# A gated mix of sliding attention and a squared-ReLU MLP on one core: start addresses of split operands moved to 64 modulo 256

## The chip, the cores and the metric

The kernel runs on one core of one Trainium2 chip. A core has TensorE (PE in the profile, its weight loads as PEld), VectorE (DVE), ScalarE (ACT), GpSimd (POOL) and SyncE (SP, which issues the transfers). They share an on-chip memory of 128 partitions; a tile occupies the same byte range in each partition, and "start address" below is that byte offset. The metric is the device time of one execution in microseconds (us); for the kernel before it is the median of three runs.

## The reference

For a sequence of 2,048 tokens of width 448, with one head block A and one MLP block B on the same x, the reference computes

```
g = sigmoid(sum(x * gate_w))                       # one number per token
q, k, v = x @ wqkv                                 # 16 heads of 28
logits  = q . k over the 8 positions s, s-2, ..., s-14, scaled by 28**-0.5
a = softmax(logits) . v  @ wo
b = relu(x @ w1 + b1)**2 @ w2 + b2                 # 448 -> 1792 -> 448
out = g * a + (1 - g) * b
```

All of it is in 32-bit floating point.

## The kernel before, in words

**Split operands.** Each matmul operand is split into a high part, which the matmul format holds exactly, and a low part, the rest. Each product is then three matmuls: high by high, high by low and low by high. ACT writes the high parts (a copy into the format), DVE subtracts to get the low ones. The tiles with h and l in their names are these parts: w1h and w1l, w2ah and w2al, and so on; for x, one tile holds both, the low part 2,048 bytes behind the high one.

**Side by side.** The width 448 is three blocks of 128 rows and one of 64. `side_by_side` (line 308) takes two lists of products and issues them alternately, one on partitions 0 to 63 and one on partitions 64 to 127, so that two half-height matmuls are in work at a time. Nearly all matmuls are issued at its line 315. In `nc.tensor.matmul(out, a, w)` the second argument is the stationary operand (it is loaded into the array, 128 columns) and the third is the moving one (it streams through, 448, 450 or 512 columns).

**Stages.** Tokens are in four chunks of 512.

- QKV (`qkv_first` and `qkv_two`, from line 393): for chunks 0, 1, 2, 3 in turn, x is stationary and wqkv moves, 448 columns for k and v and 450 for q (two more for the gate). Chunk 0 has a start of its own (line 402, matmuls over all 128 partitions). Results go to DRAM. Two pieces of the MLP are woven into the end of chunk 3.
- MLP: for chunks 3, 0, 1, 2 in turn (`ORDER`) and for 14 blocks of 128 hidden units taken two at a time, the h products (w1 stationary, x moving, 512 columns; `h_first`, `h_second`) and the b products (h stationary, w2 moving, 448 columns; `o_part`). For each later chunk, x is brought back from DRAM into tiles of `xpool` and one more slot in the pool `bw` (`x_reload`).
- Attention: POOL multiplies q by k and the weights by v, DVE reduces the products (the "pp" tiles of `prodp`), beside the MLP on PE.
- Output projection: the o tiles stationary, wo moving (`wo_split`, `wo_first`, `wo_second`, `wo_end`), woven into the MLP and at its end.

**Order of the work.** Instructions are put in order by a planner in Python (`Plan`) from fixed costs and due times; it knows nothing of addresses. SP issues nearly all transfers, in the planner's order.

**Where tiles lie.** Pools are laid out one behind the other in the order in which they are opened, and tiles within a pool likewise. The first tile of the pool `const` starts at byte 1,152, which is 128 modulo 256. Most tiles have a size that is a multiple of 256 bytes, so the remainder is handed on from tile to tile until a small tile of 64 or 192 bytes changes it. In the kernel before there are four such places: the gates' tile zg (192 bytes, between the pools `prodp` and `rawp`), b1z (64 bytes), and the tiles pad_a and pad_b (192 bytes each, never used). The slice `[:, 48:48 + n * P]` in `wo_split` skips 192 bytes as well. Remainders of the operands of PE, modulo 256:

| operand | role | before | after |
|---|---|---|---|
| wqkv parts | moving in QKV | 128 | 128 |
| x of chunks 0 and 2 | stationary in QKV | 64 | 64 |
| x of chunks 1 and 3 (pool xpool) | stationary in QKV | 128 | 64 |
| x of all chunks in the MLP (xpool, slot in bw) | moving in h | 128 | 64 |
| w1 and w17 parts | stationary in h | 128 | 64 |
| h parts | stationary in b | 64 | 64 |
| w2a and w2b parts | moving in b | 128 | 128 |
| o parts | stationary in the output projection | 64 | 64 |
| wo parts | moving in the output projection | 128 | 128 |

Every slice that a matmul takes begins a multiple of 256 bytes into its tile, so the remainder of the tile is that of the operand.

Of the kernel before, what the change touches and what calls it, by code (L numbers as in the profile page):

```python
# [7 lines left out]
F32 = mybir.dt.float32  # L8
F32R = mybir.dt.float32r
# [4 lines left out]
S, D, H, DH, W, F = 2048, 448, 16, 28, 8, 1792  # L14
P = 128
NS = 8
# [4 lines left out]
C = HG * DH  # L21
NF = F // P
# [15 lines left out]
PP_BUFS = 4  # L38
# [15 lines left out]
class Plan:  # L54
# [29 lines left out]
    def add(self, eng, cost, fn, *deps, prio=MID, at=0.0, port=False, move=None):  # L84
        j = Job()
        j.eng, j.cost, j.fn, j.deps, j.prio, j.port, j.move = eng, cost, fn, [d for d in deps if d], prio, port, move
        j.at, j.done, self.count = max(at, self.now), None, self.count + 1
        j.n = self.count
        self.jobs[eng].append(j)
        return j  # L90
# [88 lines left out]
def gated_mix_kernel(ctx: ExitStack, tc: tile.TileContext, xT, wqkv, w1, w2, wo, b1, b2, out):  # L179
    nc = tc.nc  # L180

    def f32(ap):
        return ap.bitcast(F32)
# [12 lines left out]
    const = ctx.enter_context(tc.tile_pool(name="const", bufs=1))  # L196
    psum = ctx.enter_context(tc.tile_pool(name="psum", bufs=1, space=bass.MemoryType.PSUM))

    w1h = const.tile([P, 3, F], F32R, name="w1h")
    w1l = const.tile([P, 3, F], F32R, name="w1l")  # L200
    w17h = const.tile([P, F // 2], F32R, name="w17h")
    w17l = const.tile([P, F // 2], F32R, name="w17l")
    NFA = NF // 2
    w2ah = const.tile([P, NFA, D], F32R, name="w2ah")
    w2al = const.tile([P, NFA, D], F32R, name="w2al")
    b2t = const.tile([P, D], F32, name="b2t")
    mask = const.tile([P, NS, W], F32, name="mask")

# [1 line left out]
    attp = ctx.enter_context(tc.tile_pool(name="attp", bufs=1))  # L210
    smp = ctx.enter_context(tc.tile_pool(name="smp", bufs=2))
    prodp = ctx.enter_context(tc.tile_pool(name="prodp", bufs=1))
    smallp = ctx.enter_context(tc.tile_pool(name="smallp", bufs=1))
    zg = smallp.tile([P, 6, NS], F32, name="zg")
    zt, gt, g1t = zg[:, 0:2], zg[:, 2:4], zg[:, 4:6]
    rawp = ctx.enter_context(tc.tile_pool(name="rawp", bufs=2, reuse_waits="tile"))
    biasp = ctx.enter_context(tc.tile_pool(name="biasp", bufs=1))
# [26 lines left out]
    def dma(fn, packets, size, *deps, prio=MID, at=0.0):  # L244
        return add(SYNC, 430.0, fn, *deps, prio=prio, at=at, move=(packets, size))
# [639 lines left out]
    def w2hl(f):  # L885
        if f < NFA:
            return w2ah[:, f], w2al[:, f]
        return w2bh[:, f - NFA], w2bl[:, f - NFA]

# [44 lines left out]
    bw = ctx.enter_context(tc.tile_pool(name="weights_b", bufs=1, reuse_waits="tile"))  # L934
    bp = ctx.enter_context(tc.tile_pool(name="phase_b", bufs=1, reuse_waits="tile"))
    w2bh = bw.tile([P, NFA, D], F32R, name="w2bh")
    w2bl = bw.tile([P, NFA, D], F32R, name="w2bl")
    woh = bw.tile([P, 3, D], F32R, name="woh")
# [6 lines left out]
    def x_reload(i, j, slot):  # L945
        c = ORDER[i]
        xt = (xpool if slot < 4 else bw).tile([P, 2, CH], F32R, tag=f"x{slot}", name=f"x{c}b_{j}")
        job = dma(lambda: nc.sync.dma_start(f32(xt), x_d[c, j]), 128, 4096, plan.after_pe(), x_stored[c][j], prio=NEXT)
        nxt[j] = (xt, slot, job)

    x_reload(1, 3, 4)
    bw.tile([P, 48], F32, name="pad_b")

# [23 lines left out]
    def fin_fetch(par, t):  # L979
        if (par, t) in half:  # L980
            fin_begin(par, t)
# [51 lines left out]
    def wo_split(par, t, hold, loads):  # L1033
        st = Wo()
        st.par, st.t = par, t
        place = "pp" if par and t % 4 else "oh"
        st.place = place
        free = part_last["oh"] if place == "oh" else reduced_all[-PP_BUFS:] + part_last["pp"]
        st.accs = accs = [Acc("m", f"a{par}_{t + r}", D, now=False) for r in range(2)]

        def parts():
            if place == "pp":
                oh, ol, o78 = (prodp.tile([P, C * W], F32R, tag="pp", name=f"o{n}{par}_{t}", bufs=PP_BUFS)[:, 48:48 + n * P]
                               for n in (6, 6, 2))
            else:
                oh, ol, o78 = (bp.tile([P, n * P], F32R, tag=tag, name=f"{tag}{par}_{t}")
                               for tag, n in (("oh", 6), ("ol", 6), ("o7", 2)))
            st.oh, st.ol = (o.rearrange("p (k t n) -> p k t n", k=3, t=2) for o in (oh, ol))
            st.o7, st.o8 = o78[:, :P], o78[:, P:]
            raw = hold[0]  # L1050
            st.full, st.last = raw[:, :6 * P].rearrange("p (k t n) -> p k t n", k=3, t=2), raw[:, 6 * P:]
            nc.scalar.activation(st.oh, st.full, AF.Copy)

        def copied(r):
            accs[r].open()
            st.pv = getattr(st, "pv", []) + [accs[r].pt.rearrange("p (k n) -> p k n", k=4)]
            nc.scalar.activation(st.pv[r][:, 0:3], st.full[:, :, r], AF.Copy)

        a = add(ACT, 847.0, parts, *loads, *free, prio=SOON)
        b = [add(ACT, 486.0, lambda r=r: copied(r), a, *accs[r].after, prio=SOON) for r in range(2)]  # L1060
        b[1].deps.append(b[0])
        c7 = add(ACT, 293.0, lambda: nc.scalar.activation(st.o7, st.last, AF.Copy), b[1], prio=SOON)
        d7 = add(ACT, 262.0, lambda: nc.scalar.activation(st.pv[0][:, 3], st.last, AF.Copy), c7, prio=SOON)
        lows = [add(DVE, 550.0, lambda r=r: nc.vector.tensor_sub(st.ol[:, :, r], st.pv[r][:, 0:3], f32(st.oh[:, :, r])),
                    b[r], prio=SOON) for r in range(2)]
        lows.append(add(DVE, 280.0, lambda: nc.vector.tensor_sub(st.o8, st.pv[0][:, 3], f32(st.o7)), d7, prio=SOON))
        if not par or t == 0:
            raw_last["ot"] = [d7]
        for r in range(2):
            fin_fetch(par, t + r)  # L1070
        st.jobs = [d7, *lows]
        accs[0].after, accs[1].after = (*st.jobs,), (*st.jobs,)
        return st
# [119 lines left out]
    for g in range(2, 2 * NF):  # L1193
        i, f = g // (NF // 2), g % (NF // 2) * 2
# [111 lines left out]
```

## Time and profile before

| | |
|---|---|
| median of the runs | 415.89 us (415.61 to 416.22, 3 runs) |
| the profiled execution | 415.95 us, its span 414.1 us |
| mean granted TensorE clock | 0.999 |
| PE busy | 408.6 us |
| POOL, DVE, ACT busy | 265.8, 258.6, 206.0 us |

The span runs from the first to the last instruction of the one profiled execution; its time holds a little more, what lies around the span. All times within the profile count from the span's start. An engine's busy time is the sum of the stretches in which it had an instruction in work; matmuls overlap, so the pace of PE is read from how many start in a stretch of time, and not from the duration of one. A row of a group gives line, engine, operation, "output<-inputs", shapes and count, then busy time and mean duration, then the idle time before. "L315" is line 315 of the kernel.

### The profile page before, as it was taken

To read this page: it belongs to the slowest core of one execution; us is meant where nothing else is said; L and a number is where in the kernel's file an instruction comes from. 1 tells how busy PE (TensorE), PEld (TensorE's weight loads), DVE (VectorE), ACT (ScalarE), POOL (GpSimd) and SP (SyncE) were. 2 spreads that over 40 slices of the span, in tenths; PEclk is the share of its full clock that TensorE was granted. 3 is DMA by queue.
4 is the path that set the end of the run, shared out by engine and by line. 5 is a ranking of instruction groups with operands and counts; after the bars stand their busy time and mean duration, and the time that the engine had idled before them with its cause. 6 is when DMAs were issued, how large, how long until landed. Compare 5 with 4: busy or idle time off the path is not lost.

```text
span 414.1 us, 9249 instructions
## 1 busy us (share of the span) xinstructions
PE 408.6 (99%) x3828; PEld 404.2 (98%) x3828; DVE 258.6 (62%) x346; ACT 206.0 (50%) x501; POOL 265.8 (64%) x165
## 2 busy tenths in 40 slices
PE   8999999999999999999999999999999999999996
PEld 7999999999999999999999999999999999999995
DVE  4514523484386768777656899786767586593453
ACT  5746766242464665444555435345615344346730
POOL 0000000876969999889999897999998975950000
PEclk9999999999999999999999999999999999999999
DMA  7999999845164433544203669663626022068404
GB/s 242 377 346 295 398 378 372 309 156 205 46 215 188 150 106 132 208 161 152 82 4 127 223 149 310 218 162 64 218 91 232 4 90 85 22 158 157 112 2 178
DMA packets 64555, 73.75 MB, mean 178 GB/s; under 512 B 32321, under 2 KB 57345, under 8 KB 64129
## 3 DMA queue, kind: packets, MB, share of 16 engines
q1 hardware_dynamic: 64224, 72.90, 53.5%
q8 instruction: 30, 0.49, 0.5%
q10 hardware_dynamic: 288, 0.26, 0.2%
q14 instruction: 13, 0.10, 0.1%
HBM read 45.71 MB, written 28.25 MB: 179 GB/s over the span
## 4 chain that ended last, share of the span: by engine, by line
PE 98%; DMA 1%; DVE 0%; ACT 0%; issue 0%
PE b L315 32%; PE h L315 32%; PE qkv L315 23%; PE a L315 7%; PE qkv L402 2%; PE a L1096 1%; DMA wqraw<-wqkv 1%; DVE bt_b L987 0%; ACT wqh L796 0%
## 5 line engine op out<-in xcount | busy, mean ns | idle before, releaser
L504 POOL TENSOR_TENSOR pp<-q,k 128x896 f32<-128x896 f32 x64 | 135.1, 2152 | 86.9 <-DMA k<-k_d 78.4
L516 POOL TENSOR_TENSOR pp<-lg,v 128x896 f32<-128x896 f32 x64 | 118.9, 1962 | 4.3 <-DVE lg L508 2.6
L315 PE MATMUL qkv<-wqh,x 64*128 64x448 f32 (+1 forms) x528 | 91.6, 362 | 0.0
L757 DVE TENSOR_TENSOR h<-h,h 128x512 fp32r<-128x512 f32 x56 | 38.7, 691 | 67.2 <-ACT h L756 66.8
L315 PE MATMUL b<-w2ah,h 64*128 64x448 f32 x448 | 78.8, 359 | 0.0
L315 PE MATMUL b<-w2bh,h 64*128 64x448 f32 x448 | 78.7, 359 | 0.0
L508 DVE TENSOR_REDUCE lg<-pp 128x32 f32<-128x896 f32 x64 | 67.5, 1077 | 14.0 <-POOL pp L504 14.0
L315 PE MATMUL qkv<-wql,x 64*128 64x448 f32 (+1 forms) x264 | 75.2, 362 | 0.0
L315 PEld LDWEIGHTS qkv<-wqh,x 64*128 64x128 f32 x528 | 74.0, 184 | 0.3
L526 DVE TENSOR_REDUCE o<-pp 128x112 f32<-128x896 f32 x64 | 67.2, 1069 | 3.1 <-POOL pp L516 3.1
L315 PEld LDWEIGHTS b<-w2ah,h 64*128 64x128 f32 x448 | 63.8, 184 | 0.0
L315 PEld LDWEIGHTS b<-w2bh,h 64*128 64x128 f32 x448 | 62.9, 184 | 0.2
L315 PE MATMUL b<-w2al,h 64*128 64x448 f32 x224 | 63.1, 358 | 0.0
L315 PE MATMUL b<-w2bl,h 64*128 64x448 f32 x224 | 62.3, 358 | 0.0
L753 ACT ACTIVATE h<-h,b1z 128x512 f32<-128x512 f32 x56 | 36.7, 656 | 41.1 <-PE h L315 41.1
L315 PEld LDWEIGHTS qkv<-wql,x 64*128 64x128 f32 x264 | 44.7, 184 | 0.2
L315 PEld LDWEIGHTS b<-w2al,h 64*128 64x128 f32 x224 | 38.4, 184 | 0.0
L315 PEld LDWEIGHTS b<-w2bl,h 64*128 64x128 f32 x224 | 37.7, 184 | 0.1
L315 PE MATMUL h<-x,w1h 64*128 64x512 f32 x168 | 35.7, 386 | 0.0
L315 PE MATMUL h<-x0b,w1h 64*128 64x512 f32 x168 | 35.6, 386 | 0.0
L337 ACT ACTIVATE st<-qkv 128x448 f32<-128x448 f32 x48 | 24.4, 541 | 21.8 <-PE qkv L315 15.8
L755 ACT ACTIVATE h<-h 128x512 fp32r<-128x512 f32 x56 | 33.5, 598 | 1.5
(132 smaller groups left out, 855.6 us busy)
## 6 DMA issues: line engine op xcount, KB each, us to landing
k<-k_d SPq DMA_DIRECT2D x8, 840.0 KB, 6.1
v<-v_d SPq DMA_DIRECT2D x8, 840.0 KB, 4.7
x_d<-x SPq DMA_DIRECT2D x12, 512.0 KB, 6.4
q_d<-st SPq DMA_DIRECT2D x8, 448.0 KB, 4.8
k_d<-st SPq DMA_DIRECT2D x8, 448.0 KB, 4.7
v_d<-st SPq DMA_DIRECT2D x8, 448.0 KB, 5.5
q<-q_d SPq DMA_DIRECT2D x8, 448.0 KB, 3.3
o_d<-o SPq DMA_DIRECT2D x16, 224.0 KB, 2.2
```

The source lines that it names most:

```text
L315: nc.tensor.matmul(acc.pt[:, :acc.n], a[rows], w[rows], start=acc.todo == acc.all, stop=acc.todo == 1)
L337: nc.scalar.activation(st[0][:, :, t % 2], pt[:, :D].rearrange("p (g c) -> p g c", g=G), AF.Copy)
L402: nc.tensor.matmul(acc.pt[:, :NQ], a, w, start=k == j == 0, stop=False)
L504: nc.gpsimd.tensor_mul(pr.rearrange("p (w c) -> p w c", w=W), q[:, s:s + 1].to_broadcast([P, W, C]), k[:, s:s + W])
L508: nc.vector.tensor_reduce(lgs[i][:, s], pr.rearrange("p (w h d) -> p w h d", w=W, h=HG), axis=AX.X, op=ALU.add)
L516: nc.gpsimd.tensor_mul(pr.rearrange("p (h d w) -> p w h d", h=HG, w=W), lgs[i][:, s][:, :, :, None].to_broadcast([P, W, HG, DH]), vs[i][:, ...
L526: nc.vector.tensor_reduce(o_t[par, s][:, g * C:(g + 1) * C], pr.rearrange("p (c w) -> p c w", w=W), axis=AX.X, op=ALU.add)
L753: a = add(ACT, 656.0, lambda pt=pt, r=r: nc.scalar.activation(pt, pt, AF.Relu, bias=b1t[:, f + r:f + r + 1]), ready, bias_job[0], prio=NEXT)
L755: b = add(ACT, 600.0, lambda pt=pt, hh=hh: nc.scalar.activation(hh, pt, AF.Square), a, prio=NEXT)
L757: low = add(DVE, 690.0, lambda pt=pt, hh=hh, hl=hl: nc.vector.tensor_sub(hl, pt, f32(hh)), a, prio=NEXT)
L1096: nc.tensor.matmul(acc.pt[:, :D], a, w, start=False, stop=acc.todo == 1)
```

## The change

The first half of w2 (w2ah, w2al) is allocated ahead of w1, and the gates' tile zg right behind it, in the pool const; the pool smallp goes. w2a still starts at 128 modulo 256. All that follows in const, xpool, attp, smp and prodp starts 192 bytes further modulo 256, at 64 (a few small tiles of smp at 64 or 192), up to where zg was; from the pool rawp on, everything lies where it lay. Among what moves are w1h, w1l, w17h, w17l, b2t, the mask, the x tiles of chunks 1 and 3 and of the reloads, and the tiles of q, k, v, the logits and the products. In the pool bw the unused pad_b is allocated ahead of the extra x slot and not behind it, so that this slot too starts at 64. The slice in `wo_split` starts at 0 and not at 48, since its tile starts at 64 already. No instruction is added or taken away.

```diff
+    NFA = NF // 2
+    w2ah = const.tile([P, NFA, D], F32R, name="w2ah")
+    w2al = const.tile([P, NFA, D], F32R, name="w2al")
+    zg = const.tile([P, 6, NS], F32, name="zg")
     w1h = const.tile([P, 3, F], F32R, name="w1h")
     w1l = const.tile([P, 3, F], F32R, name="w1l")
     w17h = const.tile([P, F // 2], F32R, name="w17h")
     w17l = const.tile([P, F // 2], F32R, name="w17l")
-    NFA = NF // 2
-    w2ah = const.tile([P, NFA, D], F32R, name="w2ah")
-    w2al = const.tile([P, NFA, D], F32R, name="w2al")
     b2t = const.tile([P, D], F32, name="b2t")
...
-    smallp = ctx.enter_context(tc.tile_pool(name="smallp", bufs=1))
-    zg = smallp.tile([P, 6, NS], F32, name="zg")
...
+    bw.tile([P, 48], F32, name="pad_b")
     x_reload(1, 3, 4)
-    bw.tile([P, 48], F32, name="pad_b")
...
-                oh, ol, o78 = (prodp.tile([P, C * W], F32R, tag="pp", name=f"o{n}{par}_{t}", bufs=PP_BUFS)[:, 48:48 + n * P]
+                oh, ol, o78 = (prodp.tile([P, C * W], F32R, tag="pp", name=f"o{n}{par}_{t}", bufs=PP_BUFS)[:, :n * P]
```

## The prediction

> **What bounds the kernel now.** I read the page first: the busy shares, the clock row and the chain that ended last.
>
> ```profile
> span 414.1 us, 9249 instructions
> ...
> PE 408.6 (99%) x3828; PEld 404.2 (98%) x3828; DVE 258.6 (62%) x346; ACT 206.0 (50%) x501; POOL 265.8 (64%) x165
> ...
> PEclk9999999999999999999999999999999999999999
> ...
> PE 98%; DMA 1%; DVE 0%; ACT 0%; issue 0%
> PE b L315 32%; PE h L315 32%; PE qkv L315 23%; PE a L315 7%; PE qkv L402 2%; PE a L1096 1%; DMA wqraw<-wqkv 1%; DVE bt_b L987 0%; ACT wqh L796 0%
> ```
>
> The chain is matmuls nearly throughout, at the full granted clock. Next the waits of PE alone:
>
> ```profile
> PE warm L771 <- DVE b1z L768: 1.1, 1, 1.1
> PE qkv L402 <- ACT wqh L796: 0.3, 1, 0.3
> ```
>
> PE waited 1.4 us for others, all at the start. So only the pace of the matmuls themselves can move the time. The chain in order of time (start, length, what) gives that pace:
>
> ```profile
> 304.78 2.40 PE b L315 x24
> 307.18 2.04 PE h L315 x18
> 309.22 2.40 PE b L315 x24
> 311.62 2.72 PE h L315 x24
> ```
>
> Matmuls go two side by side, one on partitions 0-63 and one on 64-127; I call the two a pair. A b pair (448 moving columns) takes 2.40 / 12 = 200.0 ns, an h pair (512 columns) 2.72 / 12 = 226.7 ns. The 64 further columns cost 26.7 ns, so 0.417 ns each; 448 columns make 186.7 ns and 512 make 213.3 ns, and both kinds carry the same 13.3 ns beside their columns.
>
> The change moves only addresses, so I looked for matmuls that are alike in all but the address. The QKV stage has them: chunks 0 and 2 have their x at 64 modulo 256, chunks 1 and 3 at 128, and the moving operand (wqkv) is at 128 for all four. I cut windows at each chunk's first matmul, for the tile qkv (columns: busy and count of PE, weight loads, ACT; clock; DMA share; GB/s). The counts include three or four matmuls in flight at the edges; by the program chunks 1 and 2 have 252 matmuls each, chunk 3 has 228 in its window and 12 in each of the two short ones.
>
> ```profile
> 31.04:56.78 25.74, 25.74 (x256) 25.63 (x253) 7.91 (x28) 1.00 1.01 355
> 56.78:82.15 25.37, 25.37 (x254) 24.93 (x253) 7.81 (x28) 1.00 0.97 347
> 82.15:105.54 23.39, 23.39 (x230) 23.34 (x226) 6.72 (x25) 1.00 0.50 169
> 108.28:109.52 1.24, 1.24 (x11) 1.21 (x11) 0.15 (x1) 1.00 0.48 160
> 114.28:115.52 1.24, 1.24 (x12) 1.21 (x11) 0.00 (x0) 1.00 0.00 0
> ```
>
> Per pair: chunk 1 25.74 / 126 = 204.3 ns, chunk 2 25.37 / 126 = 201.3 ns, chunk 3 23.39 / 114 = 205.2 ns and 1.24 / 6 = 206.7 ns. Chunk 0, once its data is there, runs at 200.0: 17 steps from the first to the second of these rows of the timeline take 3.40 us.
>
> ```profile
> 24.24 0.43 PE L315 MATMUL qkv<-wqh,x 64*128 64x448 f32 x2
> 27.64 0.43 PE L315 MATMUL qkv<-wql,x 64*128 64x448 f32 x2
> ```
>
> So x at 128 costs 3 to 6.7 ns a pair. DMA is not the reason: chunks 1 and 2 have the same DMA share (1.01 and 0.97) and differ, and chunk 3 is slow at 0.50 and at 0.00.
>
> **The change part by part.** No instruction is added, removed or reordered, on any engine or DMA queue; no wait is added. Only start addresses change.
>
> *x1 and x3 in the QKV stage, 128 to 64.* They become what x0 and x2 are. Chunk 1 goes from 25.74 to 25.37 us: -0.37. Chunk 3's 114 pairs at chunk 2's 201.3 ns take 22.95 instead of 23.39: -0.44. The two short pieces hold only 448-column pairs: 6 x 200.0 = 1.20 each instead of 1.24: -0.08. Sum -0.89 us, all of it on the path. Bounds: if every pair took 200.0 (25.20, 22.80, 1.20), -0.54 - 0.59 - 0.08 = -1.21. Chunk 2's excess of 0.17 us over 200.0 comes with its 450-column matmuls, which go at 200.0 in one stretch (12 steps in 2.40 us between these two rows) and not in others:
>
> ```profile
> 58.99 0.36 PE L315 MATMUL qkv<-w7l,x 64*128 64x450 f32 x1
> 61.39 0.36 PE L315 MATMUL qkv<-w7l,x 64*128 64x450 f32 x1
> ```
>
> If 48 pairs of a chunk paid 6.7 ns for them, the excess would be 0.32 us and the gain -0.22 - 0.27 - 0.08 = -0.57. I take -0.89, the measured neighbour.
>
> *w1 and w17 in h, stationary, 128 to 64; and at the same time x in h, moving, 128 to 64.* The counts of one chunk's h:
>
> ```profile
> L315 PE MATMUL h<-x0b,w1h x168: 385/386/386, 170.7 to 233.5; 64*128 64x512 f32 x168
> L315 PE MATMUL h<-x0b,w1l x84: 386/386/386, 170.9 to 233.2; 64*128 64x512 f32 x84
> L315 PE MATMUL h<-x0b,w17h x28: 386/386/386, 170.0 to 228.2; 64*128 64x512 f32 x28
> L315 PE MATMUL h<-x0b,w17l x14: 386/386/386, 170.3 to 228.0; 64*128 64x512 f32 x14
> ```
>
> 294 matmuls a chunk, 588 pairs in all. Today both operands have remainder 128, which costs in QKV; yet h pays the same 13.3 ns beside its columns as b, whose operands differ (64 against 128). So h shows no penalty to remove. A reading that fits: with equal remainders the load of the next weights takes up to about 206.7 ns, which is over the 200.0 of a 448-column pair and under the 226.7 of a 512-column pair, so h hides it. After the change the remainders are again equal (64 and 64), so I take 0. No row has a moving operand at 64, so it is bounded by the neighbours. Below: 450 columns at 200.0 leave 12.5 ns beside the columns, 0.8 less, 588 x 0.83 = -0.49 us. Above: the worst QKV penalty, 6.7 ns a pair, +3.92 us; its half, 3.3 ns (near chunk 1's average), +1.96 us. I take 0 as nearest to h's own rows.
>
> *b and a.* w2a moves to the front but stays at 128, h and the o tiles stay at 64; dropping the 48-column slice in the product tiles leaves the o tiles at the very byte where they were, since the pool moves up by those 192 bytes. 0.
>
> *Transfers into moved tiles: reloads of x, loads of q, k and v.*
>
> ```profile
> L948 SPq DMA_DIRECT2D x1b<-x_d x4: 320/320/384, 181.9 to 233.2; - x4
> L315 PE MATMUL h<-x1b,w17h x28: 386/386/393, 237.0 to 311.9; 64*128 64x512 f32 x28
> DMA to landing us min/median/max: 4.4/5.2/5.7
> ```
>
> The last reload is issued at 233.2 and lands by 238.9; PE starts on that x at 237.0 with other pieces, and the last piece is wanted nine pairs on, at 239.0. [...]
>
> *POOL, DVE and ACT on moved tiles.*
>
> ```profile
> L504 POOL TENSOR_TENSOR pp<-q,k x64: 2117/2146/2211, 73.6 to 326.4; 128x896 f32<-128x896 f32 x64
> 358.78 9.20 POOL L516 TENSOR_TENSOR pp<-lg,v 128x896 f32<-128x896 f32 x5
> 385.70 2.40 PE a L315 x24
> ```
>
> The eight products of a head group read q and k at steps of 448 bytes, so through all four multiples of 64 modulo 256, and stay within 2117 to 2211 ns. POOL ends at 368.0; the output projection that needs its last results runs on PE from 385.7. 0; if all 128 products took 2% more (the spread about the median), 128 x 0.04 = 5 us of those 17.7 would go.
>
> **Sum.** The profiled execution took 415.95 us (span 414.1 and 1.85 around it): 415.95 - 0.89 = 415.06. The median of the runs, 415.89, is 0.06 below it, so I predict 415.0.
>
> [...]
>
> **The rivals.**
>
> *1. h turns slower (ends above before).* If a moving operand at 64 is what hurts against a stationary one at 64, the 588 h pairs pay 3.3 ns (415.0 + 1.96 = 417.0) or 6.7 ns (418.9). For: equal remainders do cost in QKV, and no moving operand is at 64 today. Against: h has equal remainders now and pays nothing. It decides from 0.89 / 588 = 1.5 ns a pair.
>
> *2. The change does nothing.* x1 and x3 live in another pool than x0 and x2, and the two pairs differ in distance to the weights as well as in the remainder; the cause could be there. Then 415.9. For: only two chunks on each side. Against: b reads w2 from two far places (w2a and w2b, 100 KB apart) at one pace:
>
> ```profile
> L315 PE MATMUL b<-w2ah,h 64*128 64x448 f32 x448 | 78.8, 359 | 0.0
> L315 PE MATMUL b<-w2bh,h 64*128 64x448 f32 x448 | 78.7, 359 | 0.0
> ```
>
> [...]
>
> *3. h also gains.* Its 13.3 ns become 12.5: 415.0 - 0.49 = 414.5. For: the 450-column stretch at 200.0. Against: hundreds of 448-column pairs keep to 13.3 with operands at 64 and 128, so the pace looks stepped.
>
> **How the numbers follow.** Forecast 0.58, rival 1 0.20 (half at each price), rival 2 0.12, rival 3 0.07, the rest (a late reload, another coupling) 0.03. A measurement of this kernel can tell about 0.2%, 0.83 us, from no change. The forecast's own range is 415.89 - 1.21 = 414.7 to 415.89 - 0.57 = 415.3, so 0.83 lies inside it; I give three fifths of it to more than 0.2%. Faster: 0.35 + 0.07 = 0.42. Same: 0.23 + 0.12 + 0.01 = 0.36. Slower: 0.20 + 0.02 = 0.22. The range reaches from rival 3 (414.4) past rival 1's lower price (417.1) and leaves out its upper one and the rest, 0.13.
>
> **What would show it.** Right: the chunk 1 and 3 windows shrink to 25.4 and 22.9 us, the short pieces to 1.20, h stays at 2.72 for 24 and b at 2.40, PE's waits stay at 1.4 us. Rival 1: h pieces of 24 at 2.76 to 2.80. Rival 2: the chunk windows as before. Rival 3: h at 2.71. The prediction is wrong at its root if chunks 1 and 3 keep their pace, or if h pairs move off 226.7 ns.

## The result, and the profile after

The changed kernel takes 416.94 us (median, 416.83 to 417.54), the kernel before, run beside it, 415.88 us: a ratio of 1.0027, with an interval of 1.0018 to 1.0036. The forecast was 415.0 us, so the sign is wrong: the change costs 1.1 us. The profiled spans say the same, 415.2 against 414.1 us.

From the page of the changed kernel: span, busy time, the shares of the chain that ended last. (Line numbers are one less than before: L314 is the old L315.)

```profile
span 415.2 us, 9249 instructions
...
PE 409.8 (99%) x3828; PEld 404.5 (97%) x3828; DVE 254.4 (61%) x346; ACT 206.0 (50%) x501; POOL 269.3 (65%) x165
...
PE 98%; DMA 1%; DVE 0%; ACT 0%; issue 0%
```

The waits of PE in the changed kernel (what it waited for, us in total, times, longest):

```profile
PE warm L770 <- DVE b1z L767: 1.1, 1, 1.1
PE qkv L401 <- ACT wqh L795: 0.2, 1, 0.2
```

PE is still the chain nearly throughout and, after 1.3 us at the start, waits for nobody. What changed is again the pace of the matmuls. The five QKV windows of the changed kernel, cut at the same matmuls as in the prediction (chunks 1, 2 and 3, then the two short pieces):

```profile
30.97:56.36 25.39, 25.39 (x255) 25.34 (x253) 7.87 (x28) 1.00 1.02 355
56.36:81.88 25.52, 25.52 (x255) 24.76 (x253) 7.81 (x28) 1.00 0.98 349
81.88:105.00 23.12, 23.12 (x229) 22.03 (x227) 6.70 (x25) 1.00 0.53 171
107.69:108.93 1.24, 1.24 (x12) 1.21 (x11) 0.15 (x1) 1.00 0.51 170
113.69:114.92 1.23, 1.23 (x11) 1.21 (x11) 0.00 (x0) 1.00 0.00 0
sum 76.50, PE 76.50 PEld 74.55 ACT 22.53; mean PE 15.30 PEld 14.91 ACT 4.51
```

The same sum before:

```profile
sum 76.98, PE 76.98 PEld 76.32 ACT 22.61; mean PE 15.40 PEld 15.26 ACT 4.52
```

QKV did get shorter: chunk 1 by 0.35 us (25.74 to 25.39), chunk 3 by 0.27 (23.39 to 23.12). Chunk 2, whose operands did not move, got 0.15 us longer. Together -0.48 us. Chunk 0 took 0.12 us less in this profile (25.92 against 26.04), but over the profiles of all the kernels below, each with a difference of -64 there, it takes 25.8 to 26.7 us. So the loss lies in the MLP and is larger than 1.1 us.

The MLP repeats in blocks of two hidden units: 42 h matmuls and 48 b matmuls, so 21 and 24 pairs. At the steady paces of before that is 21 x 226.7 + 24 x 200.0 = 9.56 us. The chain in order of time (start, length, what) shows the same block in both kernels; a block goes from one "x22" row of h to the next. Before:

```profile
227.90 2.49 PE h L315 x22
...
231.82 1.81 PE h L315 x16
...
233.86 3.40 PE b L315 x34
...
237.46 2.49 PE h L315 x22
```

After:

```profile
228.05 2.52 PE h L314 x22
...
232.00 1.84 PE h L314 x16
...
234.07 3.41 PE b L314 x34
...
237.68 2.52 PE h L314 x22
```

Before, 237.46 - 227.90 = 9.56: the ideal, nothing is lost. After, 237.68 - 228.05 = 9.63 (9.626 by the trace's finer starts). The two h pieces take 0.03 us more each, whether they have 22 matmuls or 16, and b 0.01. A slower pace would cost 22 matmuls more than 16; this is a fixed loss at the start of a stretch. The single starts show it. These are the starts of the low-part h matmuls of one half of the array; three pairs lie between two rows, 3 x 226.7 = 0.68 us. Timeline of before:

```profile
227.62 0.39 PE L315 MATMUL h<-x0b,w17l 64*128 64x512 f32 x1
...
228.30 0.39 PE L315 MATMUL h<-x0b,w1l 64*128 64x512 f32 x1
...
228.98 0.39 PE L315 MATMUL h<-x0b,w1l 64*128 64x512 f32 x1
...
229.66 0.39 PE L315 MATMUL h<-x0b,w1l 64*128 64x512 f32 x1
```

After:

```profile
227.76 0.39 PE L314 MATMUL h<-x0b,w17l 64*128 64x512 f32 x1
...
228.46 0.39 PE L314 MATMUL h<-x0b,w1l 64*128 64x512 f32 x1
...
229.15 0.39 PE L314 MATMUL h<-x0b,w1l 64*128 64x512 f32 x1
...
229.82 0.39 PE L314 MATMUL h<-x0b,w1l 64*128 64x512 f32 x1
```

Before: 0.68, 0.68, 0.68. After: 0.70, 0.69, 0.67. The stretch starts slowly and is then back at the old pace. By the trace's starts in nanoseconds, the first five h pairs of a stretch take 231, 236, 228, 233 and 231 instead of 226.7, the first b pair 207 instead of 200, and all others are as before: 33 ns lost for an h stretch and the stretch behind it. By the starts, all 52 h stretches that come behind b or behind the output projection pay this: 52 x 0.033 = 1.7 us. (The first three, woven into the end of QKV, do not come behind either.) Where the output projection, whose remainders are those of b, stands next to b, nothing is lost. So the MLP grew by some 1.7 us, and -0.48 - 0.12 + 1.7 = 1.1 us is the difference of the spans.

### The profile page after: what moved, and what is told of

Read it like the earlier page. It is cut to its first block, busy times and chain, and to the rows that moved or that the text cites. A ratio compares the mean times of both kernels' runs of the same rounds, so it can differ in the third digit from the quotient of the medians.

```text
span 415.2 us, 9249 instructions
## 1 busy us (share of the span) xinstructions
PE 409.8 (99%) x3828; PEld 404.5 (97%) x3828; DVE 254.4 (61%) x346; ACT 206.0 (50%) x501; POOL 269.3 (65%) x165
## 4 chain that ended last, share of the span: by engine, by line
PE 98%; DMA 1%; DVE 0%; ACT 0%; issue 0%
PE b L314 32%; PE h L314 32%; PE qkv L314 23%; PE a L314 7%; PE qkv L401 2%; PE a L1095 1%; DMA wqraw<-wqkv 1%; DVE bt_b L986 0%; ACT wqh L795 0%
## 5 line engine op out<-in xcount | busy, mean ns | idle before, releaser
L314 PE MATMUL qkv<-wqh,x 64*128 64x448 f32 (+1 forms) x528 | 91.1, 361 | 0.0
L314 PE MATMUL b<-w2ah,h 64*128 64x448 f32 x448 | 83.4, 359 | 0.0
L314 PE MATMUL b<-w2bh,h 64*128 64x448 f32 x448 | 83.3, 359 | 0.0
L314 PEld LDWEIGHTS qkv<-wqh,x 64*128 64x128 f32 x528 | 74.3, 184 | 1.0
L314 PE MATMUL qkv<-wql,x 64*128 64x448 f32 (+1 forms) x264 | 74.7, 360 | 0.0
L314 PE MATMUL b<-w2al,h 64*128 64x448 f32 x224 | 71.2, 359 | 0.0
L314 PE MATMUL b<-w2bl,h 64*128 64x448 f32 x224 | 70.3, 359 | 0.0
L314 PEld LDWEIGHTS b<-w2ah,h 64*128 64x128 f32 x448 | 66.8, 184 | 0.0
L314 PEld LDWEIGHTS b<-w2bh,h 64*128 64x128 f32 x448 | 65.2, 184 | 0.2
L314 PEld LDWEIGHTS qkv<-wql,x 64*128 64x128 f32 x264 | 45.5, 184 | 0.5
L314 PEld LDWEIGHTS b<-w2al,h 64*128 64x128 f32 x224 | 41.1, 184 | 0.0
L314 PEld LDWEIGHTS b<-w2bl,h 64*128 64x128 f32 x224 | 40.1, 184 | 0.1
L314 PE MATMUL h<-x0b,w1h 64*128 64x512 f32 x168 | 36.0, 387 | 0.0
L314 PE MATMUL h<-x,w1h 64*128 64x512 f32 x168 | 36.0, 387 | 0.0
L314 PE MATMUL h<-x1b,w1h 64*128 64x512 f32 x168 | 35.9, 387 | 0.0
L314 PE MATMUL h<-x2b,w1h 64*128 64x512 f32 x168 | 35.8, 387 | 0.0
```

What stands on the lines that cost most here:

```text
L314: nc.tensor.matmul(acc.pt[:, :acc.n], a[rows], w[rows], start=acc.todo == acc.all, stop=acc.todo == 1)
```

## The experiments

All of these kernels compute the same output from the same instructions in the same order; only places in memory differ. S is the start of the stationary operand modulo 256, M that of the moving one. The difference is S - M. "Block" is the block of two hidden units just described, read from the chain between the two rows shown. Each ratio is to runs of the kernel before made beside that kernel, with medians of 415.68 to 416.08 us, and not to the 415.88 of the first row.

| kernel | h: S, M | b: S, M | block us | chunk 1, chunk 3 us | median us | ratio to before (95%) |
|---|---|---|---|---|---|---|
| before | 128, 128 | 64, 128 | 9.56 | 25.74, 23.39 | 415.88 | 1 |
| after | 64, 64 | 64, 128 | 9.63 | 25.39, 23.12 | 416.94 | 1.0027 (1.0018 to 1.0036) |
| e1, w1 alone | 64, 128 | 64, 128 | 9.61 | 25.74, 23.39 | 417.84 | 1.0042 (1.0029 to 1.0054) |
| e2, tokens alone | 128, 64 | 64, 128 | 9.73 | 25.33, 23.12 | 420.06 | 1.0099 (1.0085 to 1.0113) |
| e3, wqkv up by 64 | 128, 128 | 64, 128 | 9.56 | 25.39, 23.12 | 415.32 | 0.9984 (0.9976 to 0.9993) |
| e4, after with w2a down by 64 | 64, 64 | 64, 64 and 64, 128 | 9.64, 9.63 | 25.33, 23.12 | 417.60 | 1.0038 (1.0024 to 1.0052) |
| e5, all down by 64 | 64, 64 | 0, 64 | 9.56 | 25.74, 23.39 | 415.81 | 0.9999 (0.9990 to 1.0008) |
| e6, b alone down by 64 | 128, 128 | 0, 64 | 9.68 | 25.62, 23.22 | 418.81 | 1.0069 (1.0056 to 1.0082) |
| e7, w1 alone up by 64 | 192, 128 | 64, 128 | 9.70 | 25.68, 23.39 | 420.49 | 1.0108 (1.0094 to 1.0122) |
| e8, b alone down by 128 | 128, 128 | 192, 0 | 9.66 | 25.70, 23.25 | 418.17 | 1.0056 (1.0039 to 1.0072) |
| e9, w1 alone by 128 | 0, 128 | 64, 128 | 9.69 | 25.92, 23.19 | 419.32 | 1.0085 (1.0070 to 1.0100) |

### One operand of h at a time

w1 alone at 64. The attention pool opens ahead of xpool, a tile of 192 bytes takes zg's old place, and the 48 spare columns of the k tiles are dropped so that xpool comes to 128, and the slice in `wo_split` starts at 48 again (the last two are not shown). Against the changed kernel:

```diff
-    xpool = ctx.enter_context(tc.tile_pool(name="xpool", bufs=1))
     attp = ctx.enter_context(tc.tile_pool(name="attp", bufs=1))
+    xpool = ctx.enter_context(tc.tile_pool(name="xpool", bufs=1))
...
+    smallp = ctx.enter_context(tc.tile_pool(name="smallp", bufs=1))
+    smallp.tile([P, 48], F32, name="pad_c")
...
-    bw.tile([P, 48], F32, name="pad_b")
     x_reload(1, 3, 4)
+    bw.tile([P, 48], F32, name="pad_b")
```

> Only w1 (stationary in h) goes to 64; x stays at 128 as stationary in QKV and moving in h. The changed kernel keeps 226.7 ns a pair inside h and 200.0 inside b, but each h stretch followed by a b stretch takes 33 ns more than before: one block of two hidden units (21 h pairs, 24 b pairs) 9.63 us instead of 9.56. Theory 1 (PE loses time when the remainder of the moving operand changes from one kind of matmul to the next): all moving operands are at 128 here, so blocks take 9.56 us and the time is that of before, 415.9. Theory 2 (w1 at 64 does it, its load starts badly after a b pair): blocks 9.63, 415.9 + 1.8 = 417.7. Theory 3 (only stationary and moving both at 64 in h): 9.56, 415.9.

The tokens alone at 64 (in QKV and in h). Against the changed kernel:

```diff
-    zg = const.tile([P, 6, NS], F32, name="zg")
     w1h = const.tile([P, 3, F], F32R, name="w1h")
...
     mask = const.tile([P, NS, W], F32, name="mask")
+    zg = const.tile([P, 6, NS], F32, name="zg")
```

> Only x goes to 64 (stationary in QKV of chunks 1 and 3, moving in h); w1 stays at 128. Theory 1 (change of the moving remainder between h at 64 and b at 128): blocks 9.63 us as in the changed kernel, QKV as there, 416.9. Theory 2 (w1 at 64): blocks 9.56, QKV gain of 0.6 us kept, 415.3. Theory 3 (both at 64): blocks 9.56, 415.3.

Measured: 417.84 and 420.06 us. Each half of the change alone costs more than both together. From the chains in order of time, first of w1 alone, then of the tokens alone (a block is from one long h row to the next):

```profile
229.01 2.75 PE h L316 x24
...
238.62 2.75 PE h L316 x24
```

```profile
229.40 2.56 PE h L314 x22
...
239.13 2.56 PE h L314 x22
```

The blocks are 9.61 (9.63 late in the kernel) and 9.73 us. Here the loss is a pace that stays: with w1 alone the h pairs go round in 229, 232 and 226 ns (228.9 on average), with the tokens alone in 231 and 236 (233.3). None of the theories that these two runs were to tell apart holds as written: theory 2 had the time of w1 alone (417.7), but by a start that is slow and not by a pace, and it had the tokens alone free of cost. Neither operand carries the cost by itself, and the two do not add. What the pair of runs does say is that the two operands of one matmul have to be looked at together.

### QKV without the MLP

A 64-byte tile ahead of the wqkv parts puts them at 192, and x0 and x2, which lie behind, at 128. All else is as before; in QKV every x is now at 128 and every wqkv at 192. Against the kernel before:

```diff
     xap = actx.enter_context(tc.tile_pool(name="phase_a_x", bufs=1, reuse_waits="tile"))
+    ap.tile([P, 16], F32, name="pad_w")
     wqh = ap.tile([P, 3, NP + 2 * D], F32R, name="wqh")
```

> The kernel before with the QKV weights at 192 and the x of chunks 0 and 2 at 128, so that x is at 128 and wqkv at 192 in all four chunks; w1, x in h and w2 stay as before (moving all at 128). If equal remainders of stationary and moving operand are what costs in QKV: chunk 1 shrinks from 25.7 to 25.4 us and chunk 3 from 23.4 to 23.0, blocks of the MLP stay at 9.56, a few changes of the moving remainder between QKV (192) and h (128) cost 33 ns each (theory 1): 415.3. If x at 128 is slow in itself: all four chunks run at 204 to 206 ns a pair, 416.5. If the place (the pool) of x1 and x3 is the cause: 415.9.

Measured: 415.32 us, a ratio of 0.9984 (0.9976 to 0.9993): less than both kernels. The windows of chunks 1 to 3, and two rows of the chain for the block:

```profile
31.06:56.45 25.39, 25.39 (x255) 25.34 (x253) 7.88 (x28) 1.00 1.02 358
56.45:81.97 25.52, 25.52 (x255) 24.77 (x253) 7.80 (x28) 1.00 0.97 343
81.97:105.09 23.12, 23.12 (x229) 22.04 (x227) 6.69 (x25) 1.00 0.53 170
```

```profile
227.40 2.49 PE h L316 x22
...
236.96 2.49 PE h L316 x22
```

The three chunks take to the hundredth what they take in the changed kernel, though there x moved to 64 and here wqkv moved to 192 and x1 and x3 stayed. So the first of the three expectations held, its 415.3 us included: QKV's time went with the difference of the two starts (-64 in both), and not with the pool or the value 64. The block is 9.56: the MLP is untouched and nothing is given back.

### b's first half at difference 0

The changed kernel with zg ahead of w2a, so that w2a too is at 64 and half of the b matmuls have S = M = 64. Against the changed kernel:

```diff
     NFA = NF // 2
+    zg = const.tile([P, 6, NS], F32, name="zg")
     w2ah = const.tile([P, NFA, D], F32R, name="w2ah")
     w2al = const.tile([P, NFA, D], F32R, name="w2al")
-    zg = const.tile([P, 6, NS], F32, name="zg")
```

> The changed kernel with w2a (moving in b for the first half of the hidden units) at 64 as well; w2b stays at 128. Theory 1: in blocks with w2a the moving operands of h and b are both at 64, so the 66 ns a block do not appear; but h parts (stationary, 64) and w2a (moving, 64) now have equal remainders with 448 columns, which in QKV cost 3.3 to 6.7 ns a pair, 80 to 160 ns for 24 pairs: blocks with w2a 9.64 to 9.72 us, blocks with w2b 9.63 as in the changed kernel, 417.1 to 418.3 in all. Theory 2 (w1 at 64): the 66 ns stay in both, blocks with w2a 9.71 to 9.79, 418 to 419.2. If equal remainders cost nothing in b: blocks with w2a 9.56 under theory 1, 416.0.

Measured: 417.60 us. The chain, over one block with w2a and one with w2b:

```profile
141.53 2.51 PE h L314 x22
...
144.26 2.22 PE b L314 x22
...
151.17 2.52 PE h L314 x22
...
160.80 2.52 PE h L314 x22
```

The time lies in theory 1's range (417.1 to 418.3), but its mechanism, a free start of h where the moving remainders are equal, does not show. With w2a, b goes on at 202.6 ns a pair on average (199, 207, 202, 203 and 202 in turn in most places) instead of 200.0, and h still starts with 231, 232, 231. So difference 0 costs b something, as it costs QKV, where pairs of the same 448 columns take 203 to 207 ns. And it does not bring back the free start of h, although h and b now have the very same S and M: equal starts alone did not make the change of kind free here.

### Is 64 a bad place, or is it the places against one another?

With the relations known to matter, two readings of the changed kernel's loss were left: a start at 64 is slow for a 512-column operand, or h and b, which alternate, no longer stand to each other as they did. Two runs tell them apart: everything 64 bytes lower (the reserved area at the bottom is made smaller), and only b's and a's operands 64 bytes lower (wqkv and the tokens of chunks 0 and 2 move with them). Both against the kernel before:

```diff
-    nc = _bacc.Bacc("TRN2", target_bir_lowering=False, num_devices=1, dynamic_dma_scratch_size=1024)
+    nc = _bacc.Bacc("TRN2", target_bir_lowering=False, num_devices=1, dynamic_dma_scratch_size=960)
```

> The kernel before with everything on SBUF 64 bytes lower (the reserved area ahead of the first tile is 960 bytes instead of 1,024): w1 and the split tokens begin at 64 modulo 256 as in the changed kernel, but w2 begins at 64 and h at 0 too, so that within every kind of matmul the stationary and the moving operand stand to each other as before, and the moving operands of h, b and a all begin at one remainder (64). Theory R (what counts is the remainder of the moving operand against that of the stationary one, and that the kinds which alternate share one remainder of the moving operand; the changed kernel loses 33 ns at each change because h moves at 64 and b at 128): a block of two hidden units stays 9,560 ns as before, the time 415.9 us. Theory S (a start at 64 is slow for a moving 512-column operand by itself, whatever the others have): the block is 9,600 to 9,626 ns, the time 416.9 to 417.9 us.

```diff
     NFA = NF // 2
+    zg = const.tile([P, 6, NS], F32, name="zg")
     w2ah = const.tile([P, NFA, D], F32R, name="w2ah")
...
+    const.tile([P, 16], F32, name="pad_1")
...
-    zg = smallp.tile([P, 6, NS], F32, name="zg")
+    smallp.tile([P, 32], F32, name="pad_2")
...
+    bw.tile([P, 16], F32, name="pad_3")
     x_reload(1, 3, 4)
-    bw.tile([P, 48], F32, name="pad_b")
+    bw.tile([P, 32], F32, name="pad_b")
...
-[:, 48:48 + n * P]
+[:, 32:32 + n * P]
```

(Of the slice in `wo_split` only the end is shown. The reserved area is 768 bytes here, a whole 256 less, to make room.)

> The kernel before with h's operands left where they are (w1 and tokens at 128, all but x0 and x2) and b's and a's 64 bytes lower, both of them: w2 and wo moving at 64, h and o stationary at 0, so that the difference within b and a is that of before. Only the remainder of the moving operand now changes from h (128) to b (64) and back. Theory R: the change itself costs, as in the changed kernel with the sign turned: 20 to 35 ns at each stretch, a block 9,600 to 9,630 ns, the time 416.9 to 417.7 us before what QKV does (there wqkv and the tokens of chunks 1 and 3 now stand as 64 and 128: +-0.9 us). Theory S (64 is slow for h's moving operand only): block 9,560 ns and 415.9 us, QKV apart.

Measured: 415.81 and 418.81 us. Chains of the first and of the second:

```profile
228.41 2.49 PE h L315 x22
...
237.97 2.49 PE h L315 x22
```

```profile
229.12 2.53 PE h L317 x22
...
233.10 1.85 PE h L317 x16
...
235.19 3.41 PE b L317 x34
...
238.80 2.53 PE h L317 x22
```

The loss comes and goes on both as theory R has it. With h at 64 and 64, as in the changed kernel, but b lowered by the same 64 bytes, the block is 9.56 and the time that of before (0.9999): a start at 64 was not slow by itself. Chunks 1 and 3 of QKV, at 64 and 64, take what they took at 128 and 128 (25.74 and 23.39 us). With h left where it was free and only b moved, the block is 9.68, although b's own pair (0 and 64) was free one run earlier and h's own pair (128 and 128) is that of before. Again the two h pieces, of 22 and of 16 matmuls, lose 0.04 each. Unlike in the changed kernel, the loss is not over after five pairs: the starts of one half's low-part h matmuls are 228.95, 229.64, 230.33 and 231.02, nine pairs in 2.07 us or 230 ns a pair, against 2.04 us and 226.7 ns before. Its size theory R had wrong: 60 ns for an h stretch with its b where I expected 20 to 35, and 418.81 us where I expected at most 417.7, QKV apart. Here b lies 64 bytes lower against h than before; in the changed kernel it lies 64 higher, and the price is 33 ns. QKV, whose chunks 1 and 3 now have a difference of +64, takes 25.62 and 23.22 us. At 0 the runs give 25.68 to 25.92 and 23.19 to 23.39, so for chunk 3 that is no different from 0.

### Does the difference set the pace of h, and how far does it go round?

w1 alone at 192 (w1 behind w2 and the attention tiles, with small tiles for the remainders, the k tiles without their spare columns, which is not shown). Against the kernel before:

```diff
+    NFA = NF // 2
+    w2ah = const.tile([P, NFA, D], F32R, name="w2ah")
+    w2al = const.tile([P, NFA, D], F32R, name="w2al")
+    const.tile([P, 16], F32, name="pad_1")
     w1h = const.tile([P, 3, F], F32R, name="w1h")
...
-    NFA = NF // 2
-    w2ah = const.tile([P, NFA, D], F32R, name="w2ah")
-    w2al = const.tile([P, NFA, D], F32R, name="w2al")
...
+    attp = ctx.enter_context(tc.tile_pool(name="attp", bufs=1))
     xpool = ctx.enter_context(tc.tile_pool(name="xpool", bufs=1))
-    attp = ctx.enter_context(tc.tile_pool(name="attp", bufs=1))
+    xpool.tile([P, 32], F32, name="pad_2")
```

> The kernel before with w1 alone at 192 modulo 256 (it is allocated behind w2 and the attention tiles), the tokens still at 128: h is stationary 192, moving 128, b and QKV as before. Theory D (the pace of a 512-column pair is set by the difference stationary minus moving: 0 gives 226.7 ns, +64 gave 233.3 with stationary 128 and moving 64): h pairs at 233.3 ns, 588 x 6.7 = +3.9 us, some 419.8 us, and no further loss where b begins. Theory P (the places of the operands count one by one, and it was the 64 on either side that cost in w1 alone and in the tokens alone): 226.7 ns a pair, 415.9 us.

Measured: 420.49 us. The starts of one half's low-part h matmuls, and the block:

```profile
230.07 0.39 PE L317 MATMUL h<-x0b,w17l 64*128 64x512 f32 x1
...
230.78 0.40 PE L317 MATMUL h<-x0b,w1l 64*128 64x512 f32 x1
...
231.48 0.39 PE L317 MATMUL h<-x0b,w1l 64*128 64x512 f32 x1
...
232.18 0.40 PE L317 MATMUL h<-x0b,w1l 64*128 64x512 f32 x1
```

```profile
230.40 2.57 PE h L317 x22
...
240.10 2.57 PE h L317 x22
```

0.71, 0.70, 0.70: 233.3 ns a pair at a granted clock of 0.997, where before has 226.7 at 0.999, and it stays, as theory D asked. S = 192 with M = 128 and S = 128 with M = 64 (the tokens alone, 233.3 ns at a clock of 1.000) have nothing in common but their difference of +64, and they have one pace. D's second half, no further loss where b begins, did not quite hold: b's 24 matmuls took 2.43 to 2.44 us by the trace instead of 2.42, and most blocks are 9.71 to 9.72 us by the starts where the two paces alone give 9.70. The median is 0.7 us above the expected 419.8. These losses are 28 x 0.014 = 0.4 us of it. In this profile, that of the longest of the four runs, chunk 0 also was 0.6 us longer than in that of before; that of e1 has it 0.5 us longer too and that of e5 0.4 (26.48 against 26.04), and e5's median is that of before, so no operand's place explains it.

The last two runs ask whether 128 bytes are a whole turn. First b and a 128 bytes lower instead of 64 (the tiles as in the run with 64, with the small tiles resized, zg back in its pool and 512 bytes of reserved area; the edit against that run), then w1 at 0 instead of 192 (the edit against the run with 192):

```diff
-    zg = const.tile([P, 6, NS], F32, name="zg")
+    const.tile([P, 32], F32, name="pad_0")
     w2ah = const.tile([P, NFA, D], F32R, name="w2ah")
...
-    const.tile([P, 16], F32, name="pad_1")
+    const.tile([P, 32], F32, name="pad_1")
...
+    zg = smallp.tile([P, 6, NS], F32, name="zg")
     smallp.tile([P, 32], F32, name="pad_2")
...
-    bw.tile([P, 16], F32, name="pad_3")
+    bw.tile([P, 32], F32, name="pad_3")
     x_reload(1, 3, 4)
-    bw.tile([P, 32], F32, name="pad_b")
+    bw.tile([P, 16], F32, name="pad_b")
...
-[:, 32:32 + n * P]
+[:, 16:16 + n * P]
```

> As the run in which b's and a's operands lay 64 bytes lower than before and lost 120 ns a block, but 128 bytes lower: w2, wo and wqkv moving at 0, h and o stationary at 192, h's own operands at 128. The difference within b, a and h stays that of before, and b's place against h's is now 128 away. Theory C (any change of place between h and b costs, whatever its size): a block of 9,620 to 9,700 ns, 416.9 to 419 us before QKV's part. Theory H (only the place modulo 128 counts): block 9,560 ns as before, 415.9 us before QKV's part. QKV: chunk 2 keeps its difference (192 against 0, 25.4 us); chunks 1 and 3 stand 128 apart (x at 128, wqkv at 0): as difference 0, 25.7 and 23.4 us, by H; open by C, between 25.3 and 25.8 and 23.1 and 23.5.

```diff
-    const.tile([P, 16], F32, name="pad_1")
+    const.tile([P, 32], F32, name="pad_1")
...
-    xpool.tile([P, 32], F32, name="pad_2")
+    xpool.tile([P, 16], F32, name="pad_2")
```

> The kernel before with w1 alone at 0 modulo 256 and the tokens at 128: h is stationary 0, moving 128, a difference of 128 (it was 226.7 ns a pair at difference 0, some 229 at -64, 233.3 at +64). Theory H (only the place modulo 128 counts): 226.7 ns a pair, block 9,560 ns, 415.9 us. Theory Q (the pace goes by the difference modulo 256, and 128 is as far away as it gets): 229 to 240 ns a pair, a block of 9,607 ns or more, 416.9 to 424 us.

Measured: 418.17 and 419.32 us; the blocks of the two chains:

```profile
228.70 2.77 PE h L318 x24
...
238.36 2.77 PE h L318 x24
```

```profile
229.32 2.79 PE h L317 x24
...
239.01 2.79 PE h L317 x24
```

9.66 and 9.69, where before has 9.56: theories C and Q. 128 bytes were not a whole turn, neither between the kinds nor within h. With b 128 lower, nine or ten h pairs go between 224 and 236 ns, most of them at 228 or above, and the last two of a longer stretch at 226 to 227, so this too looks like a loss at the start, though the shorter stretches of nine pairs end before it is over; with w1 at 0, h stays between 228 and 241 throughout, 232 to 233 on average. No run moved anything by 256 bytes alone, but the reserved area was 256 bytes smaller in one and 512 in another, and their untouched relations within b kept the 200.0 ns once a stretch had settled.

## Why the prediction was wrong, point by point

**What bounds the kernel: right.** PE's waits are 1.3 us after (1.4 before), and the difference is in the spacing of matmuls. No other engine, queue or transfer had a part in it: PE had no wait on POOL, DVE, ACT or a reload behind the first 5.1 us. The reloads into x1b landed 3.5 to 5.6 us after their issue, before 4.4 to 5.7. (POOL's busy time grew from 265.8 to 269.3 us and DVE's fell from 258.6 to 254.4, with the same 1.1 us of waiting of PE on DVE and none on POOL; with wqkv alone moved, which leaves their tiles in place, they are 268.0 and 254.4.)

**x1 and x3 in QKV: the mechanism was right, the size not.** The term was -0.89 us with bounds of -0.57 and -1.21; measured -0.48. Chunk 1 came to 25.39 as foreseen. Chunk 3 gave 0.27 instead of 0.44, the short pieces at most 0.01 instead of 0.04 each, and chunk 2, taken as fixed, lost 0.15. The neighbour's pace was carried over as if it belonged to the remainders alone; the runs show chunks with unchanged remainders that move by 0.1 to 0.2 us when something around them moves (below), and why is open. One count in it was off as well: the bound of -0.57 takes 48 pairs of 450 columns in a chunk where the program has 42, and with 42 it would be -0.65. Rival 2, that nothing happens, is out: moving wqkv instead of x gave the same three times.

**"w1 and w17 in h ... and at the same time x in h": the step that failed.** It read "so I take 0" on the ground that equal remainders stay equal. As a statement on the pace it held: h pairs settle at 226.7 ns after too. But the step looked at h by itself. In the MLP h alternates with b every 18 to 24 matmuls, and the change moved h's operands against b's. Each h stretch with the stretch behind it then loses 33 ns, 1.7 us in all, and that turned -0.6 (chunk 0's 0.12 included) into +1.1. The run with b lowered along with h (block 9.56) and the run with b lowered alone (9.68) show that it is the place of one kind against the other that brings this loss. I had quoted the rows that held the answer: h and b alternating at exactly 2.72, 2.40, 2.04, 2.40 means that nothing at all is lost at a change of kind, which was a property to protect, not a given.

**The reading behind it fell as well.** I supposed that equal remainders delay the load of the next weights up to 206.7 ns and that a 512-column pair hides it. No run shows this: in QKV the weight loads of wqh are recorded at 184 ns in the mean both before and after, while chunk 1 went from 25.74 to 25.39 us. If it were so, any other relation should have been free for h. It is the reverse: at difference 0 an h pair takes 226.7 ns, and at -64, +64 and 128 it takes 229, 233.3 and some 232.5 ns. A b pair of 448 columns took 200.0 ns at -64 and 202.6 at 0.

**Rival 1 had the time but not the mechanism.** Its lower price, 417.0 us, is within 0.1 of the measured 416.94, but it was a slower steady pace, with h pieces of 24 at 2.76 to 2.80. After the change only the first five pairs of a stretch are slow, and from the sixth on h is back at 226.7 ns; that the sum of these small losses came out at rival 1's price is luck. Rival 3, h gaining, is out: in no kernel did h settle under 226.7.

**What stays open.** The runs give the relations and their prices, not the memory behind them. Why a stretch of the changed kernel needs five pairs to settle, why the two directions cost 33 and 60 ns, and what of S and M carries the change of kind was not settled: with the free relations within h and b kept, S and M move together. The other runs lean to M. With w1 alone at 192 or 0, h and b have one M and different S, and the block is within 0.02 us of the sum of its paces; with b alone moved, M differs as well and the block is 0.10 to 0.12 above. But the first half of e4, with one M and one S, is some 0.04 above.

## What to carry to other kernels

Here, with two half-height matmuls side by side and PE the bound, the start addresses of both operands were part of the pace: 226.7 to 233.3 ns for a pair of h. Where a kernel looks like this one, read the pace per pair from the chain, and compare kinds by the difference of the two starts and by the place of alternating kinds against each other. Modulo 256 is the measure used here: slices that lie multiples of 256 bytes apart in one tile went at one pace before (226.7 ns in h, 200.0 in b). A move that left the difference within each kind as it was still cost 60 ns for an h stretch with its b (b alone down by 64, block 9.68), and everything down by 64 cost nothing (9.56). So move what alternates together, or move the one stage that stands alone, as the 64-byte tile ahead of wqkv did here for 0.5 us (spans of 413.6 against 414.1). When a chain's pieces add up to exactly their steady paces, as 9.56 us did here, any edit upstream of that stage in the pools is a risk to be priced: of the ten kernels with moved tiles, eight have blocks 0.05 to 0.17 us longer.

## What the hardware showed that I had not expected

- Of the differences tried, the cheapest was not the same for h and for b. For h, which moves 512 columns, it was 0 (226.7 ns; 228.9 at -64, 233.3 at +64, some 232.5 at 128). For b, which moves 448, it was -64 (200.0 ns; 202.6 at 0), and QKV's pairs of 448 columns took 203 to 207 at 0. Whether it is the length that decides, no run tells.
- In the changed kernel a stretch of h and the stretch of b behind it lost 33 ns, in the first five h pairs and the first b pair; behind those, both kept their old paces of 226.7 and 200.0 ns. With b alone lower by 64 and by 128 the two stretches lost some 60 and 50 ns (blocks of 9.68 and 9.66), over nine pairs of h or more.
- Equal remainders did not fix a time. In two of the runs that moved only w1, QKV had the remainders of before, and still chunks 1 and 3 took 25.68 and 23.39 us in one, 25.92 and 23.19 in the other, against 25.74 and 23.39 before. From the run with w1 at 0:

```profile
30.80:56.72 25.92, 25.92 (x255) 25.37 (x253) 7.91 (x28) 1.00 1.02 360
...
82.12:105.31 23.19, 23.19 (x231) 22.96 (x227) 6.72 (x25) 1.00 0.48 168
```

By the starts in the trace, the two halves of the array ran at another distance in time in that chunk 1 (the second half started some 25 ns behind the first in the median, against some 125 before); whether that distance is cause or effect no run tells.
